# Gated mix of linear and softmax attention: the front in another order, with row maxima all through it

## The chip, the cores and the metric

The kernel runs on one core of a Trainium2 chip. The metric is the device time of one execution in microseconds. A core has a matrix engine (TensorE, PE in the profile, with its weight loads as PEld), VectorE (DVE), ScalarE (ACT), GpSimd (POOL) and SyncE (SP), which here issues every transfer between DRAM and the on-chip memories SBUF and PSUM; 16 DMA engines carry them out.

## The reference

The input x has 2048 tokens of 448 features, and two attentions of 16 heads of 28 features are computed from it and mixed by a gate:

```python
g = sigmoid((x * gate_w).sum(-1, keepdims=True))
# A: linear attention; q, k, v from x @ A_wqkv, one 28x28 w_phi for each head
pq, pk = q @ w_phi, k @ w_phi
phi_q = concatenate([softmax(pq), softmax(-pq)])     # 56 features
phi_k = concatenate([softmax(pk), softmax(-pk)])
kv, z = phi_k^T @ v, phi_k.sum(tokens)
a = (phi_q @ kv / (phi_q @ z + 1e-6)) @ A_wo
# B: softmax attention; q, k, v from x @ B_wqkv
b = (softmax(q @ k^T * 28**-0.5) @ v) @ B_wo
return g * a + (1 - g) * b
```

## The kernel before

**Precision.** Matrices are float32. Where both factors of a product come from x or a weight, each is split in a high part (a cast on ScalarE) and a low part (a subtraction), and 11 matmuls stand for one product over the 448 input features (`x3`, line 100). `XH` and `XL` hold x for the whole front.

**The front**, lines 403 to 549, computes all of A, and q, k and v of B. It runs over 16 tiles of 128 tokens:

- *Weights.* `fold` (221) multiplies A's key or query weight by w_phi, so that features come from x directly. Weights live in three places of SBUF, w1 to w3, each used by several weights in turn. Raw weights and x go through staging buffers, `stage` (112); the low parts are put off in the list `lows` and run by `take_lows`.
- *Key side*, i from 0 to 15: `features1` (278) takes maximum and minimum for each head, subtracts and takes the exponential; `features2` (292) sums and normalizes; `value_a` (315) computes A's values; `kv_add` (304) adds the product of both in PSUM.
- *Query side*, q from 0 to 15 (q is i - 16): features as above, `turn` (345) transposes them, `numer` (358) multiplies them by kv, `normalize1` to `normalize4` (237 to 271) divide by the denominators, which go through DRAM to be spread over partitions, `out_a` and `out_a2` (372 to 380) project and store A's part.
- *Softmax q and k*, `proj_qk` (386): 28 units, seven groups of 128 output features times four blocks of 512 tokens. Each ends in a tile `ev` of 128 x 2 x 512 (high and low part, two buffers), stored to the DRAM scratch `q_d` and `k_d`, one tensor for each of four head groups of 112 rows, so a unit takes one to three transfers. Six units stand among the iterations q from 2 to 7, the rest in the tail after them.
- *Softmax v*, lines 535 to 548: 16 tiles, into `vb`.

**Row maxima.** Softmax needs the maximum of each score row before its exponential. `mx_unit` (153) computes one of 256 pieces: four matmuls of 28 rows write 128 x 2048 scores to two PSUM tiles, and two reductions on VectorE (line 178) leave maxima in `part`. Every 16th unit ends with a reduction over `part`, a transpose and a negation (`mx_done`, 186). The rows come back from scratch by `mx_query` (four transfers) and `mx_load` (16). In the front a unit follows each projection from the 17th on and each softmax value tile: 28 in all.

**Attention**, lines 684 to 712: 256 steps, one for each of 16 pairs of head group and query block, times 16 key tiles. A step has four score matmuls (574), four exponentials on ScalarE (577) and eight matmul records with the values (589). The remaining units are spread evenly over the first 231 steps (`MX_STEPS`, line 700); after them the scores go two by two ("wide") through the PSUM that the units used. The last head group also projects.

**Order.** The order on TensorE, VectorE, ScalarE and GpSimd is the order in which the program writes the instructions. SP's is made by a planner from the dependences and its own estimates. PSUM is shared by tags: `s` has three slots (projections, values, features, score matmuls), `mx` two (units, `turn`, `numer`), `pv` one.

Of the kernel before, what the change touches and what calls it, by code (L numbers as in the profile page):

```python
# [29 lines left out]
EARLY = 6  # L30
# [10 lines left out]
def gated_mix_kernel(ctx, tc, xT, wqkB, wvB, wvA, wkAT, wqAT, phi, woA, woB,  # L41
# [30 lines left out]
    q_d = scratch("qd", [GW, 2, S])  # L72
    k_d = scratch("kd", [GW, 2, S])
# [15 lines left out]
    wqA_s = front.tile([P, 2, 4, 450], F32R, tag="w3", name="wqA_s")  # L89
    wp_s = ExitStack()  # L90
    wp = wp_s.enter_context(tc.tile_pool(name="wp", bufs=1))
    wkA_s = wp.tile([P, 2, 4, 512], F32R, tag="w1", name="wkA_s")
    wvA_s = wp.tile([P, 2, 4, 512], F32R, tag="w2", name="wvA_s")
    stg = wp_s.enter_context(tc.tile_pool(name="stg", bufs=3))
# [17 lines left out]
    def stage(shape_b, n, src, nm, pool=None, tag="stg"):  # L112
        raw = (pool or stg).tile([P, 2, 512], F32, tag=tag, name=nm, bufs=2 if pool else None)
        nc.sync.dma_start(raw[:, :shape_b, :n], src)
        return raw[:, :shape_b, :n]
# [7 lines left out]
    def weight_part(w, src, n, nm, b, parts=2, low=nc.vector, **at):  # L123

        bs = slice(b, b + parts)
        raw = stage(parts, n, src[:, bs, :], f"{nm}_raw{b}", **at)
        nc.scalar.copy(w[:, 0, bs, :n], raw)
        lows.append(lambda: low.tensor_sub(w[:, 1, bs, :n], raw, f32(w[:, 0, bs, :n])))  # L128


    mxs = {"u": 0}
    nm_of = {}
    acts = []

# [11 lines left out]
    def mx_load(g):  # L146
        mxs[("kc", g)] = [mx_rows("kc", f"kc{g}_{b}", k_d[g], b * 512, 6) for b in range(4)]
# [4 lines left out]

    def mx_unit():
        u = mxs["u"]
        if u >= NU:
            if u == NU:
                mx_done(NG * NQ - 1)
                mxs["u"] = u + 1
            return
        mxs["u"] = u + 1  # L160
        gq, r = divmod(u, 16)
        g, qb = divmod(gq, NQ)
        qt, kb = divmod(r, 4)
        if r == 0:
            mxs["part"] = mxp.tile([P, 16, 4], F32, tag="part", name=f"part{gq}", bufs=2)
        if r == 4 and gq + 1 < NG * NQ:
            mx_query(gq + 1)
        if r == 8 and qb == NQ - 1 and g + 1 < NG:
            mx_load(g + 1)
        qc, kc, part = mxs[("qc", gq)], mxs[("kc", g)][kb], mxs["part"]  # L170
        pm = [ps_mx(f"pm{u}_{i}") for i in range(2)]
        for j in range(4):
            js = slice(32 * j, 32 * j + DH)
            nc.tensor.matmul(pm[j // 2][:, j % 2, :], qc[js, qt * P:(qt + 1) * P], kc[js, :],  # L174
                             start=True, stop=True, tile_position=(32 * j, 0))
        p4 = part.rearrange("p (h t) k -> p h t k", t=4)
        for i in range(2):
            nc.vector.tensor_reduce(p4[:, 2 * i:2 * i + 2, qt, kb], pm[i], AX.X, ALU.max)  # L178
        if r == 15:
            red = mxp.tile([P, 16], F32, tag="red", name=f"red{gq}", bufs=2)  # L180
            nc.vector.tensor_reduce(red, part, AX.X, ALU.max)
            mxs["red"] = red
        if r == 0 and gq:
            mx_done(gq - 1)

    def mx_done(gq):
# [3 lines left out]
        nm_of[gq] = nm = mxp.tile([16, P], F32R, tag="nm", name=f"nm{gq}", bufs=5)  # L190
# [3 lines left out]
    ta_s = ExitStack()  # L194
    ta = ta_s.enter_context(tc.tile_pool(name="ta", bufs=1))
    bd = ta_s.enter_context(tc.tile_pool(name="bd", bufs=1))
    bk_s = ExitStack()
    bk = bk_s.enter_context(tc.tile_pool(name="bk", bufs=1))
    woA_s = ta.tile([P, 2, 4, D], F32R, name="woA_s")
    KV = ta.tile([112, 8, 64], F32, name="KV")  # L200
# [3 lines left out]
    def split_x(t0, n):  # L204
        tt = slice(t0, t0 + n)
        for b in (0, 2):
            raw = stage(2, n, xT[:, b:b + 2, tt], f"xraw{t0}_{b}")
# [13 lines left out]
    def fold(src, dst, nm, g):  # L221

        if g == 0:
            wts[nm] = ta.tile([112, NG, 512], F32, tag="fT", name=f"wt{nm}", bufs=1)
            for k in range(NG):
                nc.sync.dma_start(wts[nm][:, k, :], src[:, k, :])
# [36 lines left out]
    def normalize4(pool, oU, nm, n):  # L263

        oTn = []
        for k in range(n):
            oT = pool.tile([P, 2, 512], F32R, tag="oT", name=f"oT{nm}_{k}", bufs=2)
# [10 lines left out]
    def features1(pp, nm):  # L278

        p3 = pp[:, :D].rearrange("p (h f) -> p h f", f=DH)  # L280
        ext = bd.tile([P, 2, H], F32, tag="ext", name=f"ext{nm}", bufs=3)
        nc.vector.tensor_reduce(ext[:, 0, :], p3, AX.X, ALU.max)
        nc.vector.tensor_reduce(ext[:, 1, :], p3, AX.X, ALU.min)
        f = bd.tile([P, H, 2, DH], F32, tag="feat", name=f"feat{nm}", bufs=4)
        nc.vector.tensor_tensor(f[:, :, 0, :], p3,
                                ext[:, 0, :].unsqueeze(2).to_broadcast([P, H, DH]), ALU.subtract)
        nc.vector.tensor_tensor(f[:, :, 1, :],  # L287
                                ext[:, 1, :].unsqueeze(2).to_broadcast([P, H, DH]), p3, ALU.subtract)
        nc.scalar.activation(f, f, AF.Exp)  # L289
# [11 lines left out]
    pkv = ps_pv("pkv")  # L301
    fk, va, fq, fT_of, num, oTs = {}, {}, {}, {}, {}, {}
# [26 lines left out]
    def kv_copy():  # L329

        kvT = ta.tile([P, 2, 512], F32, tag="oU", name="kvT", bufs=2)[:, 0, :448]
# [39 lines left out]
    def out_a(t):  # L371
# [3 lines left out]
                        for x in out_passes(oTs[tb][g // 2], g % 2 * 256 + tl * P, woA_s, g)])  # L375
# [8 lines left out]
    UNITS = [(m, t) for m in (0, 3, 4, 1, 2, 5, 6) for t in range(NQ)]  # L384

    def proj_qk(n, ev):
# [9 lines left out]
        r = 0  # L396
        while r < P:
            G, o = divmod(m * P + r, GW)
            n = min(P - r, GW - o)
            dst = (q_d[G] if G < NG else k_d[G - NG])  # L400
            nc.sync.dma_start(dst[o:o + n, :, tt], f32(e[r:r + n]))
            r += n

    nc.sync.dma_start(phi_s, phi)
    for g in range(NG):
        fold(wkAT, wkA_s, "k", g)
        if g == 0:
            split_x(0, 256)
    weight_part(wvA_s, wvA, 450, "wvA", 0, pool=ta, tag="oU")
    weight_part(wvA_s, wvA, 450, "wvA", 2, pool=ta, tag="oU")  # L410
    split_x(256, 256)
    nc.sync.dma_start(sel_s, sel)
    nc.sync.dma_start(mask_s, mask)
    for v in vap:
        nc.gpsimd.memset(v[:, :, 28:32], 0.0)
        nc.gpsimd.memset(v[:, :, 28:29], 1.0)

    take_lows()
    ev = None
    nb = 0  # L420
    for i in range(2 * NT + 9):
# [3 lines left out]
        if i in (1, 4, 7):  # L425
            split_x(512 * (i + 2) // 3, 512)
        if y >= 2 and y - 2 < NT:
            turn(y - 2)
        if y >= 7 and y % 2 and tb - 3 < 8:
            oTs[tb - 3] = normalize4(ta, num.pop(tb - 3), f"a{tb - 3}", 2)  # L430

        if 0 <= t - 1 < NT:
# [3 lines left out]
        if t < NT:  # L436
            pk = ps_s(f"pk{t}")
            tok_major(pk, t, wkA_s, D)
            fk[t] = features1(pk, f"k{t}")
            value_a(t)  # L440
        if 0 <= q < NT:
            pq = ps_s(f"pq{q}")
            tok_major(pq, q, wqA_s, D)
            fq[q] = features1(pq, f"q{q}")
# [3 lines left out]
        if i in (8, 10):  # L448
            weight_part(woA_s, woA, D, "woA", i - 8)
        if q in (0, 1, 3, 5):  # L450
            k, b = divmod((0, 1, 3, 5).index(q), 2)
            if b == 0:
                wB[k] = wp.tile([P, 2, 4, 512], F32R, tag=f"w{k + 1}", name=f"wB{k}")
            n = 512 - 128 * k
            weight_part(wB[k], wqkB[:, :, 512 * k:512 * k + n], n, f"wB{k}", 2 * b, low=nc.gpsimd)
        if t % 2 and 0 <= t - 3 < NT:
            kv_add(t - 3)
            kv_add(t - 2)
        if 3 <= i < 7:
            fold(wqAT, wqA_s, "q", i - 3)  # L460
        if q == 5:
            gates()
        if q == 1:
            kvT = kv_copy()
            bk_s.close()
            ev_s = ExitStack()
            ev = ev_s.enter_context(tc.tile_pool(name="ev", bufs=2, reuse_waits="tile"))
        if q == 3:
            kv_out(kvT)
        if 2 <= q < 2 + EARLY or y > NT:  # L470
            for _ in range(1 if q < NT else 2):
                if nb >= 16:
                    take_acts()
                    mx_unit()
                proj_qk(nb, ev)
                nb += 1
                if nb == 12:
                    mx_load(0)
                    mx_query(0)
        if y >= 3 and y % 2 and tb - 1 < 8:  # L480
            numer(tb - 1)
        if 0 <= y - 7 < NT:
            out_a(y - 7)
        if y >= 6 and y % 2 == 0 and tb - 3 < 8:
            num[tb - 3] = normalize3(*num[tb - 3], 2)
        if y >= 4 and y % 2 == 0 and tb - 2 < 8:
            num[tb - 2] = normalize2(ta, *num[tb - 2], f"a{tb - 2}", 2, True)
    wvB_s = front.tile([P, 2, 4, 450], F32R, tag="w3", name="wvB_s")
    while nb < 28:
        if nb in (22, 24):  # L490
            weight_part(wvB_s, wvB, D, "wvB", nb - 22)
        proj_qk(nb, ev)
        take_lows()
        nb += 1
        take_acts()
        mx_unit()
    ev_s.close()
# [32 lines left out]
    vb = at.tile([P, NT, H, 32], F32, name="vb")  # L530
    nc.gpsimd.memset(vb[:, :, :, 28:32], 0.0)
    nc.gpsimd.memset(vb[:, :, :, 28:29], 1.0)
# [247 lines left out]
```

## Time and profile before

| | us |
|---|---|
| median of 3 runs | 1131.28 (1130.89 to 1134.61) |
| the profiled execution | 1134.75 |
| its span, first to last instruction | 1133.0 |
| first matmul on x | 11.6 |
| first query features | 99.7 |
| last softmax projection ends, softmax values begin | 304.8 |
| first score matmul of attention | 355.8 |
| last narrow step begins, units end | 1042.4 |

The profile gives, for each group of instructions, a count, the busy time and the mean duration, and for stretches of the span the busy time of each engine. The chain of work is followed back from the last instruction; its pieces have a start and a length.

### The profile page before, as it was taken

Reading aid. Unit: us, or ns where it says so; the run is one execution under the profiler, and the core shown is the slowest. Engines: PE = TensorE matmul, PEld = TensorE weight load, DVE = VectorE, ACT = ScalarE, POOL = GpSimd, SP = SyncE. Lnnn points to the kernel's source line nnn. Section 1 sums busy time; section 2 is a strip of 40 time slices with the busy share of each in tenths; the row PEclk is TensorE's granted clock in tenths of the full one; section 3 lists DMA queues with packets and bytes.
Section 4 is the critical chain, followed back from the end, with each engine's and each line's share of the span. In section 5 each row is a group of like instructions: output and inputs, shape, how many; then the busy total and the mean of one; then the engine's idle time right before and its main releaser. Section 6 shows DMA issues by size and latency. Waiting matters only on the chain.

```text
span 1133.0 us, 16253 instructions
## 1 busy us (share of the span) xinstructions
PE 1101.1 (97%) x6360; PEld 570.8 (50%) x6360; DVE 796.7 (70%) x853; ACT 694.4 (61%) x1226; POOL 173.7 (15%) x135
## 2 busy tenths in 40 slices
PE   7998999999999999999999999999999999999997
PEld 7887788777675333333333333333333344444444
DVE  5787567326887888888888887888888877756003
ACT  4433445522124777777777777777777767666773
POOL 2344334300250000000000000000000002020300
PEclk9999899999999999999999999999999999999999
DMA  6120332256563421225231313232112512122211
GB/s 211 61 69 7 115 112 73 96 183 196 145 136 82 123 52 59 71 53 126 60 76 38 84 52 86 77 94 51 54 52 62 124 51 76 43 80 83 89 43 66
DMA packets 61957, 96.58 MB, mean 85 GB/s; under 512 B 15176, under 2 KB 23224, under 8 KB 61880
## 3 DMA queue, kind: packets, MB, share of 16 engines
q1 hardware_dynamic: 61880, 95.54, 30.5%
q8 instruction: 50, 0.82, 0.3%
q14 instruction: 27, 0.22, 0.1%
HBM read 66.56 MB, written 28.57 MB: 84 GB/s over the span
## 4 chain that ended last, share of the span: by engine, by line
PE 82%; DVE 6%; DMA 5%; ACT 3%; issue 1%; SPq 1%; POOL 0%; ACTq 0%; DVEq 0%; POOLq 0%
PE st L574 28%; PE pv L589 22%; PE pm L174 11%; PE pqk L98 3%; PE pvb L98 3%; PE pob_False L98 3%; PE sw L574 2%; DMA kd<-ev 2%; PE poa L98 2%; PE pk L98 2%; PE pva L98 2%; PE pob_True L98 1%; PE pq L98 1%; DVE part L178 1%; DMA xraw<-in_xT_dram 1%
## 5 line engine op out<-in xcount | busy, mean ns | idle before, releaser
L178 DVE TENSOR_REDUCE part<-pm 128x2 f32<-128x1024 f32 x512 | 603.0, 1220 | 141.8 <-PE pm L174 141.7
L577 ACT ACTIVATE p<-st 128x512 f32<-128x512 f32 x924 | 501.9, 596 | 173.7 <-PE st L574 168.1
L574 PE MATMUL st<-qst,kst 128*128 128x512 f32 x924 | 347.7, 451 | 2.8 <-ACT p L577 2.3
L589 PE MATMUL pv<-p,vb 128*32 128x512 f32 x2048 | 273.4, 605 | 0.0
L574 PEld LDWEIGHTS st<-qst,kst 128*128 128x128 f32 x924 | 141.6, 187 | 252.8 <-ACT p L577 231.9
L174 PE MATMUL pm<-kc,qc 28*128 28x512 f32 x1024 | 151.3, 496 | 3.8 <-DVE part L178 3.7
L174 PEld LDWEIGHTS pm<-kc,qc 28*128 28x128 f32 x1024 | 67.9, 181 | 99.0 <-DVE part L178 50.1
L260 POOL TENSOR_TENSOR oUb<-oUb,rsb 128x512 f32<-128x512 f32 x15 | 19.2, 1283 | 453.6 <-DMA rsb<-rdb 281.0
L589 PEld LDWEIGHTS pv<-p,vb 128*32 128x32 f32 x2048 | 40.5, 108 | 89.7 <-issue 88.0
L98 PE MATMUL pqk<-XH,wB 128*128 128x512 f32 x224 | 72.8, 409 | 7.5 <-POOL wB L128 5.5
L579 ACT ACTIVATE p<-sw 128x1024 f32<-128x1024 f32 x50 | 49.3, 1024 | 22.3 <-PE sw L574 22.3
L395 DVE TENSOR_TENSOR ev<-pqk,ev 128x512 fp32r<-128x512 f32 x28 | 19.3, 691 | 50.3 <-ACT ev L394 49.6
L98 PEld LDWEIGHTS pqk<-XH,wB 128*128 128x128 f32 x224 | 41.7, 191 | 20.4 <-POOL wB L128 6.6
L394 ACT CAST ev<-pqk 128x512 fp32r<-128x512 f32 x28 | 16.3, 583 | 55.0 <-PE pqk L98 31.6
L289 ACT ACTIVATE featk<-featk 128x896 f32<-128x896 f32 x16 | 15.2, 953 | 51.7 <-DVE featk L287 51.7
L289 ACT ACTIVATE featq<-featq 128x896 f32<-128x896 f32 x16 | 15.2, 953 | 49.8 <-DVE featq L287 49.8
L98 PE MATMUL poa<-woA_s,oTa 128*128 128x448 f32 x192 | 42.7, 370 | 0.6 <-POOL oTa L269 0.6
L98 PE MATMUL pk<-wkA_s,XH 128*128 128x448 f32 x128 | 38.3, 379 | 2.8 <-ACT wkA_s L234 1.2
L98 PE MATMUL pvb<-wvB_s,XH 128*128 128x448 f32 x128 | 39.2, 388 | 0.0
L98 PEld LDWEIGHTS poa<-woA_s,oTa 128*128 128x128 f32 x192 | 35.3, 188 | 6.6 <-issue 1.5
L98 PE MATMUL pq<-wqA_s,XH 128*128 128x448 f32 x128 | 38.5, 384 | 0.0
L269 POOL TENSOR_TENSOR oTb<-oUb,oTb 128x512 fp32r<-128x512 f32 x15 | 19.3, 1284 | 118.4 <-ACT oTb L268 118.4
(121 smaller groups left out, 968.3 us busy)
## 6 DMA issues: line engine op xcount, KB each, us to landing
qst<-qd SPq DMA_DIRECT2D x64, 224.0 KB
kst<-kd SPq DMA_DIRECT2D x64, 224.0 KB
od<-oTb SPq DMA_DIRECT2D x12, 512.0 KB
oL<-od SPq DMA_DIRECT2D x12, 512.0 KB
rsa<-rda SPq DMA_DIRECT2D x16, 256.0 KB
rsb<-rdb SPq DMA_DIRECT2D x15, 256.0 KB
qc<-qd SPq DMA_DIRECT2D x64, 56.0 KB
kc<-kd SPq DMA_DIRECT2D x64, 56.0 KB
```

What stands on the lines that cost most here:

```text
L98: nc.tensor.matmul(dst, l, r, start=i == 0, stop=i == len(todo) - 1)
L174: nc.tensor.matmul(pm[j // 2][:, j % 2, :], qc[js, qt * P:(qt + 1) * P], kc[js, :], start=True, stop=True, tile_position=(32 * j, 0))
L178: nc.vector.tensor_reduce(p4[:, 2 * i:2 * i + 2, qt, kb], pm[i], AX.X, ALU.max)
L260: (nc.gpsimd if n == 1 else nc.vector).tensor_mul(oU, oU, rs)
L269: nc.gpsimd.tensor_sub(oT[:, 1, :], oU[:, k, :], f32(oT[:, 0, :]))
L289: nc.scalar.activation(f, f, AF.Exp)
L394: nc.scalar.copy(e[:, 0, :], pq)
L395: nc.vector.tensor_sub(e[:, 1, :], pq, f32(e[:, 0, :]))
L574: nc.tensor.matmul(st, kst_of[(g, kt // 4)][:, j, (kt % 4) * P:(kt % 4 + 1) * P], qst_of[gq][:, j, :], start=True, stop=True)
L577: nc.scalar.activation(p[:, jl, :], st, AF.Exp, scale=SCALE)
L579: nc.scalar.activation(p, sts, AF.Exp, scale=SCALE)
L589: nc.tensor.matmul(pv[32 * j:32 * j + 32, :], vb[:, kt, 4 * g + j, :], pt[j // 2][:, j % 2, :], start=kt == 0, stop=kt == NT - 1, tile_pos ...
```

## The change

The front is put in another order. All 28 softmax projections come first, in an order that begins with the four groups of the first token block; their weight is loaded in columns of 128. A's key weight is folded between the last eight of them. Then follow the key side, the query side and ten of the 16 softmax value tiles; the first six value tiles stand in the last iterations of the query side. Row-maximum units stand at the last eight projections, in three of four iterations of the key side, in each iteration from q = 1, once more in the last five, and at the ten value tiles. The scratch of q and k becomes one tensor, so that a unit is stored by one transfer. Features are copied to SBUF once by ScalarE; both reductions read the copy, both subtractions move to GpSimd, and the exponential is issued an iteration later. `normalize3` and `normalize4` come an iteration sooner. `mx_load` loads one block at a time. Attention itself is unchanged.

The core of the diff:

```diff
-    q_d = scratch("qd", [GW, 2, S])
-    k_d = scratch("kd", [GW, 2, S])
+    qk_d = dr.tile([2 * D, 2, S], F32, tag="qkd", name="qkd")
+    q_d = [qk_d[g * GW:(g + 1) * GW] for g in range(NG)]
+    k_d = [qk_d[D + g * GW:D + (g + 1) * GW] for g in range(NG)]
...
+        if r >= 12 and qb == NQ - 1 and g + 1 < NG:
+            mx_load(g + 1, kb)
...
     def features1(pp, nm):
-        p3 = pp[:, :D].rearrange("p (h f) -> p h f", f=DH)
+        pc = bd.tile([P, H, DH], F32, tag="pc", name=f"pc{nm}", bufs=2)
+        nc.scalar.copy(pc, pp[:, :D].rearrange("p (h f) -> p h f", f=DH))
...
-        nc.vector.tensor_reduce(ext[:, 0, :], p3, AX.X, ALU.max)
-        nc.vector.tensor_reduce(ext[:, 1, :], p3, AX.X, ALU.min)
+        nc.vector.tensor_reduce(ext[:, 0, :], pc, AX.X, ALU.max)
+        nc.vector.tensor_reduce(ext[:, 1, :], pc, AX.X, ALU.min)
...
-        nc.vector.tensor_tensor(f[:, :, 0, :], p3,
-                                ext[:, 0, :].unsqueeze(2).to_broadcast([P, H, DH]), ALU.subtract)
...
-        nc.scalar.activation(f, f, AF.Exp)
+        nc.gpsimd.tensor_sub(f[:, :, 0, :], pc,
+                             ext[:, 0, :].unsqueeze(2).to_broadcast([P, H, DH]))
+        nc.gpsimd.tensor_sub(f[:, :, 1, :],
+                             ext[:, 1, :].unsqueeze(2).to_broadcast([P, H, DH]), pc)
+        exps.append(lambda: nc.scalar.activation(f, f, AF.Exp))
...
+    UNITS = ([(m, 0) for m in range(4)] + [(m, t) for t in range(1, NQ) for m in (0, 3)]
+             + [(4, t) for t in range(NQ)] + [(m, t) for m in (1, 2) for t in range(1, NQ)]
+             + [(m, t) for m in (5, 6) for t in range(NQ)])
...
+        nc.sync.dma_start(qk_d[m * P:(m + 1) * P, :, tt], f32(e))
+    ev = ev_s.enter_context(tc.tile_pool(name="ev", bufs=2))
+    stg = ev_s.enter_context(tc.tile_pool(name="stg", bufs=6))
...
+    for n in range(28):
+        take_acts()
+        if n in (0, 2, 4):
+            x_loads(n // 2 + 1)
+        if n == 6:
+            part_loads("wB1", wqkB[:, :, 512:896], 384, "wB1")
+        splits(n + 1)
+        if n == 11:
+            part_loads("wvA", wvA, 450, "wvA")
...
+        if n == 15:
+            nc.sync.dma_start(phi_s, phi)
+            load_fold(wkAT, "k")
+        if n >= 20:
+            mx_unit()
+        proj_qk(n, ev)
+        if n == 10:
+            mx_query(0)
+        if 10 <= n < 14:
+            mx_load(0, n - 10)
...
+        if n >= 20 and n % 2 == 0:
+            fold(wkA_s, "k", (n - 20) // 2)
...
+    for i in range(2 * NT + 8):
         t, q = i, i - NT
...
+        if t < NT and t % 4 < 3:
+            mx_unit()
+        while exps:
+            exps.pop(0)()
...
+        if 0 <= q < NT:
+            pq = ps_s(f"pq{q}")
+            tok_major(pq, q, wqA_s, D)
+        if q >= 1:
+            mx_unit()
...
+        if 0 <= q < NT:
+            fq[q] = features1(pq, f"q{q}")
...
+        if q >= NT + 3:
+            mx_unit()
...
+        if q >= NT + 2:
+            value_b(q - NT - 2)
+        if y >= 5 and y % 2 and tb - 2 < 8:
+            num[tb - 2] = normalize3(*num[tb - 2], 2)
...
-    for t in range(NT):
+    load_q(0)
+    for t in range(6, NT):
+        value_b(t)
         take_acts()
         mx_unit()
-        if t == 7:
-            load_q(0)
-        if t % 4 == 3:
-            load_k(0, t // 4)
+        if t < 10:
+            load_k(0, t - 6)
```

## The prediction

> **What bounds the kernel now.** I read the page first, its sections on busy time and on the chain of work that ended last:
>
> ```profile
> PE 1101.1 (97%) x6360; PEld 570.8 (50%) x6360; DVE 796.7 (70%) x853; ACT 694.4 (61%) x1226; POOL 173.7 (15%) x135
> ...
> PE 82%; DVE 6%; DMA 5%; ACT 3%; issue 1%; SPq 1%; POOL 0%; ACTq 0%; DVEq 0%; POOLq 0%
> ```
>
> TensorE is busy 97% of the span and is 82% of the chain, so time is lost or won in its work and its waits. Then I cut the span at the places where the work changes and read the busy time of each engine by stretch. The columns are the stretch, its length, busy time (and instructions) of TensorE, weight loads, VectorE, ScalarE and GpSimd, granted clock, DMA share, GB/s.
>
> ```profile
> 11.60:99.70 88.10, 85.99 (x833) 76.61 (x833) 72.42 (x114) 33.99 (x62) 30.31 (x19) 0.98 0.25 78
> 99.70:172.40 72.70, 66.63 (x415) 54.17 (x409) 45.81 (x81) 30.44 (x41) 28.95 (x18) 0.93 0.32 91
> 172.40:214.60 42.20, 40.80 (x242) 34.79 (x243) 25.90 (x45) 21.88 (x29) 20.52 (x14) 1.00 0.25 83
> 214.60:304.80 90.20, 86.13 (x396) 64.66 (x394) 45.69 (x52) 25.35 (x41) 8.01 (x7) 1.00 0.57 168
> 304.80:355.80 51.00, 49.26 (x243) 36.92 (x243) 40.56 (x38) 10.41 (x22) 22.39 (x14) 0.97 0.64 141
> 355.80:1042.90 687.10, 684.17 (x3784) 255.87 (x3784) 552.77 (x501) 513.44 (x964) 48.16 (x39) 1.00 0.27 71
> ```
>
> The first five are the front (with 11.6 us of start before them): key and value features; the query side; its steady part; the tail with most of the softmax projections; the value projection. The sixth is attention with a row-maximum unit in nearly every step. The front ends at 355.8 us, attention takes the other 777.2. The change moves 30 units from the sixth row to the front and turns the front round. All five front rows are nearly full of TensorE too, so a unit moved there is not free.
>
> Next, TensorE's work in the front, by spacing in the timeline: 28 projections, 22 matmuls in 5.32 us for two, 28 x 2.66 = 74.5; key and value features, eight iterations from 59.50 to 99.76, 16 x 5.0 = 80; folding of one weight 4.4; query features 16 x 2.26 = 36.2; their transposes 16 x 1.04 = 16.6; numerators 8 x 1.88 = 15; output projection 16 x 2.47 = 39.5; softmax values 16 x 2.25 = 36; 28 units of 0.5 (0.43 between projections, 0.67 between value tiles: 2.92 against 2.25) = 14. That is 316 us, with the start 328, so some 28 us are waits. I find 10 of them at 108 to 122 (the wait for a weight's low part and the half clock after it), 3.5 in the first eight key iterations (47.9 us, of which 4.4 is folding), 2 at 250, 4 at 284 to 300, 4 around 332 to 342 for the last weight, and 2 of cold clock.
>
> **What a unit costs in attention.** In the timeline one step of group 1 has no unit. Columns: start, length, engine, line, operation.
>
> ```profile
> 682.43 1.06 PE L589 MATMUL pv<-p,vb 128*32 128x512 f32 x8
> ...
> 685.37 1.06 PE L589 MATMUL pv<-p,vb 128*32 128x512 f32 x8
> ...
> 687.97 1.06 PE L589 MATMUL pv<-p,vb 128*32 128x512 f32 x8
> ...
> 690.73 1.06 PE L589 MATMUL pv<-p,vb 128*32 128x512 f32 x8
> ```
>
> Steps with a unit alternate between 2.94 and 2.76 (mean 2.85); the one without is 2.60. So a unit taken out saves 0.25 us, not its 0.5: the four exponentials of a step, 0.55 apart, hold the rest. In the last group, where output projections fill TensorE (steps of 3.7), it saves up to 0.45. The new front issues 8 + 12 + 28 + 10 = 58 units, so 199 calls instead of 229 are spread over the same 231 steps. **Gain:** 25 x 0.25 + 5 x 0.45 = 8.5 us (7.5 if all save 0.25; 13 if all save 0.45).
>
> **What the front gains and pays.**
>
> Added TensorE work: 30 units x 0.5 = +15 (13 to 20). Folding the key weight was hidden in the start, while x was on its way; now it stands between projections, four times 1.1 = +4.4. The start keeps its length: x arrived at 8.4 to 9.6 us, after 1.6 MB; now 1.3 MB must land, and a cast of 1.06 and a low part of 2.2 follow: the first unit ends near 14 us, where 11.6 + 2.66 would put it (-2 to +2).
>
> Waits that go: the 10 at 108 to 122 (that weight is now needed at the very start), 3.5 in the key features (x's low parts, 2.2 us of VectorE each, move to the first stage), 2 and 4 in the tail: -19.5 (-15 if some return). The 4 at the last weight stay: one raw buffer and ScalarE waiting for it, as before.
>
> Waits that come:
>
> (a) *The stores of the first 28 units.* Each unit needs one of two ev buffers, free again when its 512 KB are in DRAM.
>
> ```profile
> 119.79 3.64 DMA qd<-ev
> ...
> 157.09 3.33 DMA kd<-ev
> ...
> 224.45 7.99 DMA kd<-ev
> ...
> 234.58 4.17 DMA kd<-ev
> ...
> 242.48 8.31 DMA kd<-ev
> ```
>
> These pieces of the chain (start, length) are stores from issue to landing: 3.3 to 3.6 us alone, 4.2 beside another store, 8 beside other transfers. A buffer's round is the cast 0.59, the subtraction 0.69, 0.15 of signals and the store: 5.0 to 5.6 us, over two buffers 2.5 to 2.8 a unit against TensorE's 2.66. There is no slack, and in the first 20 units (53 us) the DMA also carries the rest of x (3.1 MB), three weights (2.8) and the kc and qc rows (1.1). From 240 to 270 us 5.7 MB kept the DMA engines 62% busy for 30 us, 3.25 us a MB: those 7 MB are 23 us, besides 33 us for 20 stores. Together they fill the 53 us. A transfer in front of a store lengthens the round of both buffers, half of it a unit: 23/2 = 11.5, less what falls into gaps and less one unit that three PSUM slots let TensorE run ahead: **+8** (0 to 18). The kc loads also wait on SP for the store just issued, four issues of 0.6 each; that is inside this range.
>
> The Trainium skill, DMA: Bandwidth & Descriptors, section Rules for kernel authors, says that two transfers to disjoint sets of partitions serialize on the same engines and that one transfer of 128 partitions should be used, which is what this change does to the store. By it a store loses a second issue, 0.6 us, a round becomes 4.9, and the term would be about 5. No row here has a 128-partition store.
>
> (b) *Units between the last eight projections.* From 278.8 to 304.4 seven projections with a unit took 3.65 us each against 3.2 of work: 8 x 0.4 = **+3** (0 to 5).
>
> (c) *Key features.* The subtractions go to GpSimd. The groups of instructions (count, then busy time, mean ns) show nothing of this shape there; nearest are the product of the features and a sum of the same size:
>
> ```profile
> L298 POOL TENSOR_TENSOR featk<-featk,fsumk 128x896 f32<-128x896 f32 x16 | 27.2, 1703 | 55.2 <-DVE fsumk L297 51.7 <-PE pva L98 3.5
> ...
> L614 POOL TENSOR_TENSOR acc<-acc,ob_False 128x448 f32<-128x448 f32 x12 | 13.7, 1144 | 127.2 <-ACT ob_False L613 127.2
> ```
>
> By them a subtraction is 0.85 (half the product) to 1.14; with 1.14 GpSimd has 4.0 in an iteration of 5.3: it fits. VectorE has 2.44 for a unit in three of four iterations and 1.2 + 1.43: 4.5. But the exponential now stands ahead of the next copy on ScalarE, a ring of copy 0.53, two reductions 1.2, two subtractions 2.3, exponential 0.95 and signals 0.2: 5.2 us, just TensorE's pace. **+2** (0 to 6).
>
> (d) *Start of the query side, q from 1 to 7.* TensorE has 30.2 us there (features 7 x 2.26, units 3.5, five transposes, two numerators, and small ones), no projections any more. VectorE has 7 x (2.4 + 1.2 + 1.43 + 0.15) = 36, and 4 of gates, mask and normalizing: 40; the ring of (c) gives 36. TensorE meets a unit in each iteration and waits for its PSUM. Of 10 us VectorE can be 3 late into the longer iterations behind: **+7** (3 to 10).
>
> (e) *Rest of the query side.* TensorE 7.2 us an iteration, VectorE 6, GpSimd 5.3. The normalization is now multiplied one iteration earlier: two transfers, 1.6 and 3.5 to 7.5, must land within 7.2. Queued behind the multiplication on VectorE are the next unit's reductions, and TensorE waits for these. **+2** (0 to 6).
>
> **Sum:** 15 + 4.4 - 19.5 + 8 + 3 + 2 + 7 + 2 - 8.5 = +13.4 us, front +21.9 (378), the rest -8.5. The profiled execution, 1134.75 us with a span of 1133.0, would become about 1148; it lies 3.5 above the median 1131.28, and from the median I forecast 1131.3 + 13.4, **1145 us**.
>
> **Rivals.** *TensorE runs ahead (faster).* Three PSUM slots let it go one or two projections ahead of the engine that limits, some 5 us in each stretch, and in the steady part of the query side (172 to 215) it waits for almost nothing. If each of (a) to (e) is cut by up to 5, they are 3 + 0 + 0 + 2 + 0 = 5: net -3.6, with a gain of 13 in attention -8; about 1126. For it: 41 of 42 us busy in that stretch. Against: VectorE's sum in (d), and no slack in (a). It decides where the new waits add up to less than 8.6 us.
>
> *Stores as slow as the contended ones (slower still).* With 8 us to land, a round is 9.4, a unit 4.7: ten units beside loads lose 20 instead of 8: 1157. For it: the two 8 us rows. Against: small strided transfers and reloads were beside these, too. In the trace the wait of 4 us at 108 was followed by a clock of 0.50 for 8 us. The Trainium skill, TensorE: Matmul & The Clock Gate, section What's actually happening, has the clock halve after an idle window of about 3.4 us, and the trace agrees; waits of 2 us a unit would stay under that.
>
> *An even trade.* Front +8.5, attention -8.5: 1131. *The units do not move*: the counts in the code leave little room for it, so I give it no share.
>
> **Chances.** Forecast (1136 to 1152) 0.50, slower still 0.12, even 0.10, faster 0.28. A difference under 0.3% (3.4 us) cannot be told from none. So faster 0.28, same 0.10, slower 0.62. All best bounds together give -12, all worst +47; neither is likely, and 1121 to 1160 leaves out the outer parts of the first two and of the faster one, about 0.15.
>
> **What would show it.** Right: the first score matmul near 378 us; ev copies spaced by about 3 us, waiting for stores; TensorE idle near 200 to 235 us on VectorE's reductions; some 30 steps of 2.6 in attention. Wrong: ev spaced by 2.66; iterations q 1 to 7 below 5 us; a front under 364 us, which would make the kernel faster.

## The result and the profile after

The changed kernel takes **1187.71 us** (median of 4 runs, 1183.76 to 1188.76), the kernel before beside it 1132.29: a ratio of 1.0481 (interval 1.0449 to 1.0513). It is slower, as forecast, but by 55 us and not by 13, and outside the range of 1121 to 1160.

The page's busy times and chain of work, after:

```profile
PE 1110.8 (94%) x6360; PEld 573.4 (48%) x6360; DVE 767.0 (65%) x789; ACT 710.9 (60%) x1258; POOL 232.5 (20%) x198
...
PE 66%; DMA 4%; ACT 3%; DVE 1%; issue 1%; SPq 0%; DVEq 0%; ACTq 0%
```

TensorE's busy time grew by 10 us, the span by 54: what came is waiting. Cut at the places where the work changes (columns as before: stretch, length, busy time of TensorE, weight loads, VectorE, ScalarE, GpSimd, granted clock, DMA share, GB/s):

```profile
6.50:103.30 96.80, 88.19 (x376) 65.78 (x377) 56.64 (x63) 29.87 (x46) 6.78 (x12) 0.96 0.74 246
103.30:192.30 89.00, 89.00 (x879) 77.49 (x877) 68.46 (x92) 34.21 (x68) 53.25 (x46) 1.00 0.05 17
192.30:247.30 55.00, 39.11 (x287) 30.91 (x279) 40.37 (x56) 24.62 (x33) 36.30 (x30) 0.91 0.09 28
247.30:373.30 126.00, 111.34 (x597) 84.36 (x594) 82.99 (x96) 46.37 (x68) 57.45 (x46) 0.95 0.18 61
373.30:419.10 45.80, 31.87 (x152) 23.75 (x150) 23.60 (x23) 8.40 (x17) 16.76 (x10) 0.81 0.78 159
419.10:1096.60 677.50, 668.60 (x3660) 248.84 (x3662) 482.23 (x439) 510.05 (x962) 48.17 (x39) 1.00 0.26 70
```

These are the 28 projections; the key side; the query side up to its first output product; from there to the last ten value tiles; these tiles; attention. The prediction's terms, put together by the same stretches, against them (the first output product comes in iteration q = 8, behind a transpose, the features and a unit):

| stretch | by the prediction's terms | us | measured end or length |
|---|---|---|---|
| projections end | 11.6 + 74.5 + 8 x 0.5 + 4.4 + (a) 8 + (b) 3 | 105.5 | 103.3 |
| key side | 2 x 40.3 + 12 x 0.5 + folding 4.4 + (c) 2 | 93 | 89.0 |
| to the first output product | q 1 to 7: 30.2 + (d) 7; q = 0: some 3; q = 8: 1.04 + 2.26 + 0.5 | 44 | 55.0 |
| to the last ten value tiles | what is left of 378 | 102 | 126.0 |
| last ten value tiles | 10 x 2.92 + the 4 at the last weight | 33 | 45.8 |
| attention, to the end | 777.2 - 8.5 | 768.7 | 767.9 |

All of the miss lies in three rows: +11, +24 and +13. Attention came out as forecast; a step with no unit takes 2.62 us between two of these rows (start, length), and 2.75 to the next, which has one:

```profile
641.91 1.06 PE L671 MATMUL pv<-p,vb 128*32 128x512 f32 x8
644.53 1.06 PE L671 MATMUL pv<-p,vb 128*32 128x512 f32 x8
647.28 0.64 PE L671 MATMUL pv<-p,vb 128*32 128x512 f32 x4
```

The view of waits says who stood in those stretches (engine and line that waited, the tile and engine waited for; total us, times, longest):

```profile
DVE oUa L277 <- DMA rsa<-rda: 40.3, 8, 6.7
...
ACT ev L416 <- DMA qkd<-ev: 33.0, 13, 7.6
...
ACT oTa L285 <- DVE oUa L277: 28.5, 8, 5.5
ACT woB_s L130 <- DMA woB_raw<-in_woB_dram: 27.5, 4, 19.2
...
PE pft L372 <- DVE part L189: 16.3, 8, 5.9
```

The first is the multiplication by the spread reciprocals, which waits 5 us on average in its eight turns (12.5 us in two turns before). Behind it on VectorE stand the unit's reductions, for which TensorE waits to reuse the PSUM tiles (last line), and on ScalarE the casts of `normalize4`. The fourth is the last weight, 12.7 us before. The chain of work shows how that weight was served (start, length):

```profile
375.80 6.47 DMA qst<-qkd
382.34 8.76 DMA kst<-qkd
391.17 10.20 DMA woB_raw<-in_woB_dram
401.39 0.57 ACT woB_s L130
```

SP issues the first of its four raw parts at 374.89 and the second only at 391.17, behind twelve loads of the stacks for attention, which the short last stretch now issues in a row.

### The profile page after: what moved, and what is told of

The parts are those of the page before. It is cut to its first block, busy times and chain, and to the rows that moved or that the text cites. A ratio compares the mean times of both kernels' runs of the same rounds, so it can differ in the third digit from the quotient of the medians.

```text
span 1187.0 us, 16174 instructions
## 1 busy us (share of the span) xinstructions
PE 1110.8 (94%) x6360; PEld 573.4 (48%) x6360; DVE 767.0 (65%) x789; ACT 710.9 (60%) x1258; POOL 232.5 (20%) x198
## 4 chain that ended last, share of the span: by engine, by line
PE 66%; DMA 4%; ACT 3%; DVE 1%; issue 1%; SPq 0%; DVEq 0%; ACTq 0%
PE st L656 25%; PE pv L671 21%; PE pm L186 9%; PE pob_False L103 3%; PE sw L656 2%; PE pvb L103 2%; ACT p L659 2%; PE poa L103 1%; PE pob_True L103 1%; DMA rsa<-rda 1%; DVE part L189 1%; DMA woB_raw<-in_woB_dram 1%; DMA kst<-qkd 1%; DMA qst<-qkd 1%; DMA dena<-oUa 0%
## 5 line engine op out<-in xcount | busy, mean ns | idle before, releaser
L186 PE MATMUL pm<-kc,qc 28*128 28x512 f32 x1024 | 150.7, 499 | 19.4 <-DVE part L189 17.8
L417 DVE TENSOR_TENSOR ev<-pqk,ev 128x512 fp32r<-128x512 f32 x28 | 19.3, 691 | 37.3 <-ACT ev L416 37.2
L696 POOL TENSOR_TENSOR acc<-acc,ob_False 128x448 f32<-128x448 f32 x12 | 13.7, 1142 | 124.9 <-ACT ob_False L695 124.9
L372 PE MATMUL pft<-ident,featq 128*112 128x128 f32 x128 | 19.5, 302 | 19.5 <-DVE part L189 16.3
```

What stands on the lines that cost most here:

```text
L372: nc.tensor.transpose(pt[:112, n // 4, n % 4 * P:(n % 4 + 1) * P], f[:, n * 112:(n + 1) * 112], ident)
L417: nc.vector.tensor_sub(e[:, 1, :], pq, f32(e[:, 0, :]))
```

## The experiments

Each kernel computes the full result, and its ratio is to runs of the kernel before made beside it. The letters in the expectations stand for theories: W, E and N for the multiplication that waits for the reciprocals' load (N: moved sooner, it costs by itself), S for the last weight queued behind the stacks.

| run | us | ratio to before (interval) |
|---|---|---|
| rs_spread | 1168.02 | 1.0307 (1.0289 to 1.0326) |
| wob_early | 1173.59 | 1.0350 (1.0325 to 1.0374) |
| spread_wob | 1150.41 | 1.0160 (1.0145 to 1.0176) |
| before_norm_early | 1150.31 | 1.0150 (1.0133 to 1.0167) |
| norm_late | 1197.73 | 1.0567 (1.0549 to 1.0585) |
| all_three | 1182.32 | 1.0434 (1.0418 to 1.0450) |
| no_query_units | 1193.17 | 1.0540 (1.0524 to 1.0555) |
| late_no_units | 1182.55 | 1.0434 (1.0412 to 1.0457) |
| norm_mid | 1191.15 | 1.0498 (1.0475 to 1.0521) |
| sw_no_early_units | 1152.81 | 1.0182 (1.0164 to 1.0199) |
| sw_vector_feat | 1158.16 | 1.0217 (1.0199 to 1.0234) |
| lnu_vector_feat | 1185.58 | 1.0450 (1.0426 to 1.0474) |
| lnu_vector_feat_sw | 1164.01 | 1.0271 (1.0252 to 1.0290) |
| ev_three | 1149.15 | 1.0135 (1.0119 to 1.0151) |
| before_spread_wob | 1127.10 | 0.9938 (0.9918 to 0.9957) |

**The load of the reciprocals, faster.** `rs_spread` loads both halves by four transfers of 32 partitions instead of two whose source has four rows:

```diff
-            nc.sync.dma_start(rs[:, k, :], rd[k].unsqueeze(1).to_broadcast([4, 32, 512]))
...
+        if n == 2:
+            for j in range(4):
+                nc.sync.dma_start(rs[32 * j:32 * j + 32],
+                                  rd[:, j, :].unsqueeze(0).to_broadcast([32, 2, 512]))
```

> The changed kernel with the spread denominators (rs) loaded by four transfers of 32 partitions for both halves, instead of two transfers whose source has four rows as its outermost dimension; nothing else. Theory W with its cause E (such a transfer runs on four of the 16 DMA engines): each lands in about 4 us instead of 7, VectorE's waits for rsa<-rda fall from 5 us to 1 or 2: 12 to 20 us shorter, 1168 to 1176 us. Rival F (the 7 us are fixed cost of a round through DRAM): no change beyond 3 us, 1184 to 1191 us.

It gave 19.7 us, as theory W with its faster landing has it; rival F falls. The wait in its view of waits:

```profile
DVE oUa L282 <- DMA rsa<-rda: 18.5, 7, 4.4
```

**The last weight, earlier.** `wob_early` loads it raw in one transfer to a buffer of its own, ahead of the stacks:

```diff
+    woB_raw = at.tile([P, 4, D], F32, name="woB_raw")
+    nc.sync.dma_start(woB_raw, woB)
     load_q(0)
...
-            weight_part(woB_s, woB, D, "woB", (t - 6) // 2, 1)
+            b = (t - 6) // 2
+            split_weight(woB_s, woB_raw[:, b:b + 1, :], slice(b, b + 1), slice(0, D))
```

> The changed kernel with softmax's output weight loaded raw in one transfer into a buffer of its own, written ahead of the loads of the q and k stacks; casts and low parts stay where they are. Theory S (the weight's loads are queued behind the stack loads, ScalarE waits for them with the value copies behind it): the waits of 19.2 and 4.8 us vanish and the last ten value tiles take about 31 us instead of 45.8: 12 to 16 us shorter, 1172 to 1176 us. Rival K (the stack loads and their memsets, 21.6 us on GpSimd, bound this stretch): at most 4 us shorter.

It gave 14.1 us, as theory S has it. `spread_wob` has both edits:

> The changed kernel with both edits that helped: rs on four transfers, output weight early. If the two stretches are independent, the gains add: 19.7 + 14.1 us, 1154 us (1151 to 1157). If the faster query side only brings the stack loads forward into a stretch that bounds anyway, the sum is smaller: 1158 to 1164 us.

They add: 37.3 us, 3.5 more than the sum of the two. Its stretches from the first query features on, by the busy times:

```profile
192.40:243.90 51.50, 40.07 (x283) 30.79 (x280) 39.91 (x56) 23.64 (x32) 34.76 (x30) 0.90 0.12 30
243.90:350.90 107.00, 103.09 (x588) 79.13 (x585) 83.50 (x96) 47.16 (x69) 57.33 (x46) 1.00 0.23 72
350.90:381.90 31.00, 30.95 (x161) 23.61 (x160) 25.43 (x26) 8.36 (x17) 18.61 (x11) 1.00 0.85 189
```

The last two are 107.0 and 31.0 us long instead of 126.0 and 45.8, with TensorE busy for nearly all of it at a full clock; the table above has 102 and 33. The 55 before them are still 51.5.

**The early multiplication alone.** `before_norm_early` is the kernel before with only `normalize3` one iteration sooner, without a unit on its query side:

```diff
-        if y >= 6 and y % 2 == 0 and tb - 3 < 8:
-            num[tb - 3] = normalize3(*num[tb - 3], 2)
+        if y >= 5 and y % 2 and tb - 2 < 8:
+            num[tb - 2] = normalize3(*num[tb - 2], 2)
```

> The kernel before with the multiplication of normalize3 one iteration earlier, alone: this is the changed kernel's edit without its units on the query side. Theory W says VectorE then waits for rsa<-rda here as well, about 5 us eight times, but behind it stand only the features' reductions and nothing that TensorE needs at once: 0 to 8 us slower, 1132 to 1141 us. Rival N (the early multiplication costs by itself, whatever is queued behind it): 15 us slower or more.

18 us slower, as rival N has it, and nearly all of it ahead of attention (first score matmul at 371.9 instead of 355.8). The wait in its view of waits is of the same size as in the changed kernel:

```profile
DVE oUa L260 <- DMA rsa<-rda: 46.0, 8, 8.4
```

**The same place without units.** `no_query_units` is the changed kernel with `if q >= NT + 1` for `if q >= 1` at the query side's units; they run in attention instead.

> The changed kernel without row-maximum units in q from 1 to 16: these 16 go to attention; the early normalization and its slow transfer stay. Theory W with the units as what makes the wait costly: TensorE no longer meets a unit behind the wait: 8 us of unit work and 20 to 30 us of waits less in the front, 4 us more in attention: 1152 to 1163 us. Rival N: only 8 less and 4 more: 1180 to 1186 us.

No gain: it is 5 us slower, beyond both expectations. A pair of iterations still takes 14.9 to 16.8 us from load to load, and the chain of work shows why (start, length):

```profile
250.02 6.83 DMA rsa<-rda
...
256.94 1.24 DVE oUa L277
...
258.19 1.14 ACT oTa L285 x2
259.33 0.44 ACT pcq L298
...
259.81 3.92 PE pq L103 x11
263.73 0.88 PE poa L103 x5
264.61 0.55 ACT ga L398
...
265.17 0.32 SPq L399
...
265.60 0.53 SPq L272
...
266.18 7.48 DMA rsa<-rda
```

It is a ring. The load lands, VectorE multiplies, ScalarE casts, and only then comes ScalarE's copy that frees the feature PSUM slot; so TensorE's next query features wait, then the output product, then ScalarE's gate; and SP issues the next reciprocals' load behind the store of that gated tile. The unit is not in it. A turn later the chain closes by another way, from ScalarE's copy (292.4) through the features' reductions on VectorE to the next reciprocals and their load (297.9). So the ring has more than one way round, of about equal length. The load is the only link that a run made shorter; what the others are worth is not shown.

**One iteration later again.** `norm_late` puts `normalize3` and `normalize4` of the changed kernel back to where they were before; `all_three` adds the two edits above; `norm_mid` goes half the way (multiplication at the head of the even iteration, casts behind its features); `late_no_units` is `norm_late` without query-side units.

```diff
-        if y >= 6 and y % 2 == 0 and tb - 3 < 8:
+        if y >= 7 and y % 2 and tb - 3 < 8:
             oTs[tb - 3] = normalize4(ta, num.pop(tb - 3), f"a{tb - 3}", 2)
...
-        if y >= 5 and y % 2 and tb - 2 < 8:
-            num[tb - 2] = normalize3(*num[tb - 2], 2)
+        if y >= 6 and y % 2 == 0 and tb - 3 < 8:
+            num[tb - 3] = normalize3(*num[tb - 3], 2)
```

> The changed kernel with normalize3 and normalize4 put back one iteration later, nothing else. Theory W (VectorE waits for the transfer): in the changed kernel the multiplication by the spread denominators waits some 5 us for rsa<-rda in every second iteration, and the row-maximum reductions queued behind it hold TensorE; two iterations take 16.5 us. One iteration later the transfer (7 us from issue) has landed: these waits vanish, two iterations take their 14.4 us of TensorE work, and with the last pairs the query side gets 18 to 25 us shorter: 1163 to 1170 us. Rival L (VectorE's load: units, reductions and the rest, as the prediction had it): the waits only move to other instructions, at most 4 us shorter: 1183 to 1188 us.

> The three edits together: normalization an iteration later, rs on four transfers, output weight early. Theory W and S: the first two overlap and the third adds: 32 to 40 us shorter than the changed kernel, 1148 to 1156 us, still slower than the kernel before (1132), because some 10 us of VectorE-bound iterations at the start of the query side stay. Rival L and K: above 1178 us.

> The changed kernel with its multiplication by the reciprocal half an iteration later: not at the end of the odd iteration but at the head of the even one after it, ahead of the unit's and the features' reductions on VectorE; ScalarE's casts of it move from the head of that iteration to behind its features and gates. Nothing else differs. Theory N (the ring from reciprocal through the four-engine load, the multiplication and ScalarE's casts back to the next reciprocal sets the 16.5 us of a pair; what was taken from it is headroom): the rsa wait (40.3 us) falls to under 12 and the time to 1165-1176, as much as the faster load gave (1168). Rival P (any place of the multiplication that leaves GpSimd's low parts behind the unit and the feature product keeps out_a waiting, as with one whole iteration later): 1184-1198.

> The changed kernel with both edits at once: multiplication and casts one iteration later, as they stood in the kernel before, and no units of the row maxima beside the query side (they run in attention). Query loop's second half then holds what it held in the kernel before. Theory N' (late is good where no unit's reductions of 2.35 us stand before the multiplication): the pair of iterations falls from 18-20 us to 13.2-14, and with the units' TensorE time handed to attention the time is 1160-1172. Rival (the late place is slow in the changed kernel for another reason, such as GpSimd, which now makes the features): pairs stay above 16 us, 1185-1200.

My theory missed all four. `norm_late` is 10 us slower than the changed kernel although no wait for the load is left. `all_three` is 15.4 us under it, about what the weight alone gave, and its eight multiplications start within 0.03 us of those of `norm_late`: in this place the faster load gives nothing. From the timeline of `norm_late` (start, length, engine and line; in brackets the idle time before):

```profile
280.74 2.35 DVE L189 TENSOR_REDUCE part<-pm 128x2 f32<-128x1024 f32 x2 [8.44 <-PE pm L186]
...
285.44 1.18 DVE L277 TENSOR_TENSOR oUa<-oUa,rsa 128x1024 f32<-128x1024 f32 x1
...
285.67 2.52 POOL L316 TENSOR_TENSOR featq<-featq,fsumq 128x896 f32<-128x896 f32 x1
...
286.66 1.14 ACT L285 CAST oTa<-oUa 128x512 fp32r<-128x512 f32 x2
...
288.15 2.49 POOL L286 TENSOR_TENSOR oTa<-oUa,oTa 128x512 fp32r<-128x512 f32 x2
...
289.46 3.76 PE L103 MATMUL poa<-woA_s,oTa 128*128 128x448 f32 x10 [1.45 <-POOL oTa L286]
```

The multiplication now comes behind the unit's reductions and the features' extrema and sum; cast and low part follow directly ahead of the output product that needs them, the low part behind GpSimd's feature product. The first three pairs take 18 to 21 us, the others 15 to 19. The four corners (without units on the query side, these run in attention):

| | units on the query side | none there |
|---|---|---|
| multiplication early | 1187.7 | 1193.2 |
| multiplication late | 1197.7 | 1182.6 |

So neither place is good by itself: late is 10.6 us better where VectorE is free ahead of it and 10 worse behind a unit. Without units a late pair took 14.6 us in the middle of the loop and 13.8 to 19.4 over all of it, not the 13.2 to 14 I expected. `norm_mid` fell on its rival's side: its chain still holds loads of 6.9 to 7.7 us, one in most pairs, and then reductions, feature product and low part.

**The first 50 us of the query side.** Three runs took out what I blamed: `sw_no_early_units` is `spread_wob` without the units of q = 1 to 7, `sw_vector_feat` is `spread_wob` with the query features subtracted by VectorE from PSUM as before, and `lnu_vector_feat` is `late_no_units` with the same:

```diff
+        pc, sub = pp[:, :D].rearrange("p (h f) -> p h f", f=DH), nc.vector
+        if nm[0] == "k":
+            pc, sub = bd.tile([P, H, DH], F32, tag="pc", name=f"pc{nm}", bufs=2), nc.gpsimd
+            nc.scalar.copy(pc, pp[:, :D].rearrange("p (h f) -> p h f", f=DH))
...
-        nc.gpsimd.tensor_sub(f[:, :, 0, :], pc,
+        sub.tensor_sub(f[:, :, 0, :], pc,
...
```

> The same two edits, and no row-maximum unit in q from 1 to 7: these seven go to attention. Theory V (in these short iterations VectorE bounds, 5.2 us with a unit against 2.8 to 5.7 of TensorE; with rs on four transfers the seven iterations still take 46 us): 10 us less in the front, 2 us more in attention: 6 to 9 us shorter than the two edits alone, 1146 to 1149 us. Rival C (the ring through copy, reductions, GpSimd, exponential, 5 us, holds them): less than 3 us shorter.

> The kernel with both repairs (1150.4 us), and in it the query side's feature subtractions as in the kernel before: on VectorE, from the projection's PSUM bank, with no ScalarE copy and no GpSimd instruction; the key side stays as changed. Theory G (the query loop's remaining excess, 192 to 244 us before the first output product and 14.6 us a pair after, is a ring through GpSimd's two subtractions of 0.94, queued with its product of 1.70 to 2.5 and its low parts of 1.28 each): the first stretch falls from 51.5 to 45 or less, the time to 1138-1146. Rival V (VectorE then has 6.8 us of the 7.2 us of an iteration, units among them, and becomes the wait itself): 1150-1165.

> The kernel with multiplication and casts one iteration later and no units on the query side (1182.6 us), and in it the query side's feature subtractions back on VectorE from PSUM. Its query loop then has no edit left in it but the exponential's place, an iteration later, and the projections that are gone. Theory G: pairs fall from 14.5 to 13.2-13.6 us, the first stretch from 46.5 to 41 or less, the time to 1160-1172. Rival (GpSimd's subtractions lie beside other work, and what holds the late place is something else, such as the exponential moved behind the next iteration's turn): 1178-1188.

From the first query features to the first output product:

| | subtractions on GpSimd | on VectorE |
|---|---|---|
| units there | 51.5 (spread_wob) | 56.0 (sw_vector_feat) |
| none | 46.3 (sw_no_early_units); 46.5 (late_no_units; late multiplication) | 42.2 (lnu_vector_feat; late multiplication) |

Both theories fall as single causes. The units cost 5 us there, 3.5 of them their own TensorE work, and the GpSimd subtractions 4 without units; with units VectorE is the tighter place, and moving the subtractions back costs 4.5. None of the runs became faster as a whole. In `sw_no_early_units` the first score matmul comes 3 us sooner than in `spread_wob`, and attention, where the seven units now run, takes 3 us more. In `lnu_vector_feat` what the stretch gained came back as waits behind it. `lnu_vector_feat_sw` is this last one with the two edits of `spread_wob`:

> As the one before it (late multiplication, no query-side units, query features on VectorE), with the two repairs as well: the reciprocal's load by four transfers and the last weight loaded ahead. Late multiplication does not wait for the load, so theory N gives the load nothing here, and the weight 12-16 us: 12 to 18 under the kernel before it. If the load's landing still decides in the late place: 25 or more under it.

It gains 21.6 us, between the two expectations, and does not show that the load decides. By the two traces attention starts 22.8 us sooner. Of these, 16.2 lie behind the first softmax value tile, where the weight is, and 2.9 ahead of the query side, where neither edit acts. Of the 3.7 between, 2.6 are the first multiplication's shorter wait for its load (1.6 instead of 4.2 us). From the second multiplication on, the distances are the same to 0.1 us in both runs.

**A third buffer for the projected tiles** (`ev`, bufs 2 to 3, in `spread_wob`):

> The kernel with both repairs (1150.4 us) and a third buffer for the 28 projected tiles on their way out to memory. Theory A (the 14 us by which the first stage is longer than its TensorE work are ScalarE waiting for a store to free one of two buffers): 5 to 10 us shorter, 1140-1146. Rival D (the stores are held by the DMA engines' rate, so a third buffer only defers the wait): within 2 us, 1148.5-1152.

1.3 us, as the rival said. ScalarE's wait for the stores halves against that in `spread_wob` (35.9, 15 times), and the first stage ends 2.5 us sooner; what it gains is mostly given back later. ScalarE waits for TensorE instead. The two waits by its view of waits:

```profile
ACT ev L421 <- PE pqk L103: 40.8, 17, 6.7
...
ACT ev L421 <- DMA qkd<-ev: 16.9, 6, 7.5
```

**The two edits on the kernel before.**

> The kernel BEFORE with the two repairs that gave 37 us in the changed kernel: the reciprocal's load by four transfers of 32 partitions each, and the raw last weight loaded in one transfer to a buffer of its own ahead of the last value tiles. If the two waits that its page lists (12.5 us of VectorE for rsa, 12.7 us of ScalarE for the last weight) lie on its path: 1112-1122. Rival: its multiplication has a whole iteration more, so the load of 7 us is hidden and only the weight's waits count: 1121-1128. If neither decides there: 1130-1134.

1127.10 us, the fastest of all, 0.6% under the kernel before. The projections' last matmuls start 3.6 us sooner (300.4 instead of 304.0), and attention 7.1 (348.7 instead of 355.8): by these two traces half of the gain is the load's and half the weight's, so the rival's time was right and its reason half right.

## Why the prediction was right and wrong

**Attention, -8.5:** right; -9.3. **Terms (a), (b), (c)** and the folding: right in sum; the first two stretches ended 2 and 4 us better than their terms. The 2 are the start's: the first copy to `ev` came at 11.9 us, where the forecast had the first unit end near 14. A GpSimd subtraction took 0.94, inside 0.85 to 1.14.

The mechanism of (a) held, but in another place. TensorE stands idle for 8.6 us of the first stage (96.80 less 88.19). The waits before projections, and the longest wait of ScalarE for a store:

```profile
PE pqk L103 <- ACT XH L224: 7.6, 3, 6.5
...
PE pqk L103 <- DVE ev L417: 5.7, 2, 5.3
...
68.41 0.58 ACT L416 CAST ev<-pqk 128x512 fp32r<-128x512 f32 x1 [7.56 <-DMA qkd<-ev]
```

The 6.5 of the first line are the start, before the first matmul; the parts of x account for less than 3 of the 8.6 us. The other 5.7 wait for the subtraction into `ev`, which waits for a store: 0.5 in the first 20 units, for which (a) had 8, and 5.3 at 64.5 us, behind a store that SP issued after the loads of the key weight. A third buffer leaves 3.4 of this and ends the stage 2.5 sooner. That the rate of the transfers held the store, as the rival of that run had it, wasn't shown by itself. One reading in (a) was wrong: the page before does list a store of 128 partitions, `od<-oTb` of 512 KB in attention, though without a time to landing.

**Term (e), +2, failed**, and it is the largest part of the miss: about 20 us. It priced the load as something to land within 7.2 us and so nearly hidden. The row was right (6.8 to 7.5), but store, issue, load, multiplication and casts follow each other through engines that work in order, and come back to the next load. In the middle of the loop the ring takes 15.7 to 17.4 us, against 14.4 us of TensorE work for a pair of iterations. `before_norm_early` shows the step alone (+18), `rs_spread` takes most of it away (-19.7), and `no_query_units` shows that the units, which I had named as what queues behind it, are not what makes it long.

**"The 4 at the last weight stay" failed:** it was 14 more, which `wob_early` gave back. I counted the wait that went with 16 value tiles; the last stretch has ten, and the same loads of the stacks go ahead of the weight on SP within it.

**Term (d), +7, was mis-sized:** some 14 (the stretch is 7.5 over its terms in `spread_wob`). There TensorE is idle for 11.4 of the 51.5 us. Of these, 8.3 are waits for VectorE's reductions of the units, as (d) has it, and 3.1 are one wait of the first transpose for the first query features and ScalarE's copy of `kv`, which no term names. The other 3 us or so are work at the lower granted clock of 0.90 (an estimate: 40.07 busy, less the 37 of the terms). No single removal made the kernel faster.

Of the table's +11, +24 and +13 the two repairs give back 37; 7.5 and 5 remain in the first two of these rows. With the repairs the kernel takes 1150.4, 5 us above the forecast and in its likeliest range, but this is partly luck: the other rows are 8 us under their terms. **Of the rivals** none came; the sign of the change was right, its size was not. Of the signs, `ev` copies 3.4 us apart on average, TensorE idle at 200 to 235 us on VectorE's reductions and attention steps of 2.6 came true; none of these tests (e). The first score matmul, at 419 instead of 378, did.

## What to carry to other kernels

Where a result is taken one iteration sooner, follow it through every queue until it meets itself again: on engines that work in order, a wait that is shorter than an iteration can still set its length. Price the transfers at the end of a stage anew when the stage gets shorter, in the order of the issuing queue. And an edit that helps without one other change may hurt with it, so test both corners.

## What the runs showed of the hardware

**The same reciprocals land sooner with 32 than with 4 as the outermost count of the source.** From the last issue to landing, the 512 KB took 6.83 to 7.48 us as two transfers with four source rows (chain of `no_query_units`), and 2.88 to 3.77 as four transfers whose source begins with a count of 32 (chain of `sw_no_early_units`). Counted from the first of its issues, the load of 250.02 above took 7.4, and the one shown here 4.5. From the chain of `spread_wob`:

```profile
330.89 3.19 DMA rsa<-rda
```

The Trainium skill, DMA: Bandwidth & Descriptors, section Why a DMA increments its semaphore by 16 and not by 1, says that a transfer runs on as many engines, up to 16, as divide the slowest dimension of both its sides; by that it is four for the first kind and sixteen for the second. The times agree in direction; no view here shows which engines ran.

**A small VectorE operation can last until GpSimd's ends.** In the timeline of the changed kernel two operations of one kind stand 1.4 us apart. The first ends with the GpSimd product beside it (228.74 and 228.71):

```profile
227.01 1.70 POOL L316 TENSOR_TENSOR featq<-featq,fsumq 128x896 f32<-128x896 f32 x1
...
227.24 1.50 DVE L346 TENSOR_SCALAR gate<-gate 128x16 f32<-128x16 f32 x1
228.65 0.17 DVE L266 TENSOR_SCALAR dena<-dena 128x32 f32<-128x32 f32 x1
```

All eight of the second kind took 0.17 to 0.18 before, and up to 1.08 after. The Trainium skill, SBUF — State Buffer, section Who interferes with whom, says that `tensor_scalar` can enter a mode that takes a port pair which GpSimd shares, and that the one that comes second then blocks; the trace agrees.

**A wait can cost twice.** The same ten matmuls of an output product in `lnu_vector_feat` took 4.10 us after a wait of 3.1, and 2.33 after one of 1.1:

```profile
256.38 4.10 PE L103 MATMUL poa<-woA_s,oTa 128*128 128x448 f32 x10 [3.11 <-POOL oTa L286]
...
273.69 2.33 PE L103 MATMUL poa<-woA_s,oTa 128*128 128x448 f32 x10 [1.09 <-POOL oTa L286]
```

The granted clock of that run was 0.83 from 250 to 270 us and 1.00 from 270 to 290. In the kernel before, the wait at 108 that the prediction put at 4 us was 3.3 (until 111.32), and the clock was 0.50 from 112 to 120. By stretch it was 0.95 and 0.81 in the changed kernel's last two stretches of the front, 1.00 and 1.00 in `spread_wob`.
